# Gathered values: one kernel's V rows by indirect transfers, its weights on a second queue, and a new order

## The chip, the cores and the metric

One core of a Trainium2 chip runs the kernel. The metric is device time in microseconds (us): the median of three timed runs was 982.84 us (980.65 to 984.33). Five engines run side by side, each through its own instruction list in order: TensorE (PE, with its weight loads as PEld), VectorE (DVE), ScalarE (ACT), GpSimd (POOL) and SyncE (SP). Transfers between memory and the on-chip buffers are carried by 16 DMA engines, whichever engine's queue starts them.

## What is computed

Block-sparse attention over 4 batches, 8 heads, 768 positions and 64 channels, followed by an MLP whose gate is h * relu6(h + 3) / 6. A query block of 32 rows sees its own and the two neighbouring blocks, the first and the last block, and three sampled blocks; the first and last query blocks see everything.

```python
mask = np.abs(blk_i - blk_j) <= window                     # window = 1, blocks of 32
mask = mask | (blk_i == 0) | (blk_j == 0) | (blk_i == n_blocks - 1) | (blk_j == n_blocks - 1)
for qb in range(n_blocks):
    for kb in sampled_blocks[qb]:
        mask[qb * block:(qb + 1) * block, kb * block:(kb + 1) * block] = True
scores = np.where(mask, scale * np.matmul(q, k.transpose(0, 1, 3, 2)), -1000000000.0)
attn = softmax(scores)
x = np.matmul(attn, v)                                     # to (tokens, 512)
h = x @ w_in                                               # 512 -> 2048
out = (h * np.clip(h + 3.0, 0.0, 6.0) / 6.0) @ w_out       # 2048 -> 512
```

The weights come as 64-bit floats and the matmuls of the MLP run on a high and a low part, so each weight tile is split on the chip.

## The kernel before, in words

A long table, `SCORE`, writes the whole program out by hand: each entry names a piece of work and its step, and the steps are issued in exactly that order, on the engine that each step uses. Nothing reorders them later, so the table is the order of every queue.

The pieces are these. `k0` is the index: it loads the sampled block numbers and derives a second list for V, in which samples that repeat or lie inside the window are replaced by an empty block. `p0` to `p43` are pairs of neighbouring query blocks: `kw` and `vw` load the four window blocks of K and V, `kg` and `vg` the first and last block (only when the tile held another batch), `kr` and `vr` the six sampled blocks, each by a transfer of its own whose address SyncE takes from a register; `registers` (L342) loads six numbers into registers first. K and V tiles (`kp`, `vp`) form rings of three pairs. `q0` to `q23` load the queries of a group of blocks. `j0` to `j43` are attention jobs: `s` the scores, `mx` the row maximum, `e` the exponentials, `t` transposes, `ca`/`cv` copies, `av` the product with V, `dn`, `ml`, `x`, `xh`, `xl` the division and the split into high and low. `d0` to `d7` are the blocks that see everything, with K and V in tiles named `stage`. `w0` to `w31` are weight tiles: `load` into `stage` (a ring of three), `size` on ScalarE, three `bits` steps on VectorE, `high` on ScalarE, `low` on GpSimd or VectorE, `save` back to memory. `m0` to `m63` are MLP steps, eight units of eight: `h` (24 matmuls), `ga`, `gb`, `gh` and `gl` for the gate and its split into `ghi` and `glo`, `o` (18 matmuls into `out`). The first unit takes the low parts as they are made; later ones load them again with `loadin` and `loadout` (`wlo_in`, a ring of four, and `wlo_out`, a ring of three). After eight steps, `oc` copies and `od` stores the output.

All transfers are started by SyncE (`dma`). Attention runs ahead of the MLP by a few jobs, and both interleave with the weight work in roughly the first quarter of the time. Operations pass through one helper, so nearly every row of the trace carries line L286.

Of the kernel before, what the change touches and what calls it, by code (L numbers as in the profile page):

```python
# [17 lines left out]
P = 128  # L18
# [25 lines left out]
    t_1 ca_0; j2 x; j3 cv_1; j2 xh xl; j3 av_0 av_1 dn; p4 vw; j3 ml; p5 vw; j3 x; p4 vr; j3 xh xl; j4 s; p5 vr; j4 mx
    e_00 e_01 e_10 t_0 e_11; w0 load; j4 cv_0 t_1; w1 load; w2 load; j5 s; j4 cv_1; q3 load; p6 kw kr; j5 mx; j4 av_0;
    j5 e_00; j4 av_1; j5 e_01; j4 dn; j5 e_10 t_0; j4 ml; w0 size; j5 cv_0; j4 x; p7 kw; j5 e_11; p7 kr; w0 bits_0; j4
    xh; j5 t_1; w1 size; w0 bits_1; j5 ca_1; w0 bits_2; j4 xl; w0 high; w1 bits_0; j5 av_0; w0 low_0; w1 bits_1; j5
    av_1; w3 load; p6 vw; w1 bits_2; p7 vw; p6 vr; w2 size; j5 dn ml; w1 high; w2 bits_0; j5 x xh; w2 bits_1; w1
# [696 lines left out]
```

## Time and profile before

| | us |
|---|---|
| median of three runs | 982.84 (980.65 to 984.33) |
| profiled run | 986.81 |
| its span, first to last instruction | 985.0 |
| TensorE busy in the span | 827.3 |
| VectorE busy | 342.2 |
| ScalarE busy | 274.1 |
| GpSimd busy | 152.2 |

An engine's busy time says little by itself, since the stages differ. Which stage an engine waits in, and for whom, is read from the views below: the slices of the span, the table by stage, the chain of work that ended last (followed back from the end, at each step to what released it), and the waits. SPq is SyncE's queue, which starts transfers; "landing" is the end of a transfer.

### The profile page before, as it was taken

The numbers are of one execution on the slowest core, as the hardware profiler recorded it, in microseconds if no ns is written. First come the engines' busy times: TensorE is split into PE (matmuls) and PEld (weight loads), VectorE is DVE, ScalarE is ACT, GpSimd is POOL, SyncE is SP. The second block draws the span as 40 slices with busy tenths as digits, with TensorE's granted clock in tenths as the row PEclk, the third lists the DMA queues.
The fourth block names the chain that finished last, engine by engine and source line by source line (L and its number), as shares of the span: only waits on it lengthen the run. The fifth ranks groups of instructions, "written<-read, shape, count | busy, mean of one in ns | idle before, by whom it ended". The sixth has DMA issues, their size and how long they took to land.

```text
span 985.0 us, 20294 instructions
## 1 busy us (share of the span) xinstructions
PE 827.3 (84%) x7968; PEld 656.8 (67%) x7968; DVE 342.2 (35%) x590; ACT 274.1 (28%) x496; POOL 152.2 (15%) x93
## 2 busy tenths in 40 slices
PE   3567776687899799977998989977999888999997
PEld 1335555565787587756787767756777666778895
DVE  1336566675323143322422223322322223233111
ACT  1114434453223132322222223221232222222121
POOL 0001132231211011110111110110111110111221
PEclk9756877878799799988999989988999999999999
DMA  6557889888665765777457666777456665535441
GB/s 169 163 156 229 264 257 271 230 275 243 214 200 162 212 199 166 225 196 220 151 166 215 197 174 206 223 205 220 141 170 203 186 179 185 156 106 151 143 128 64
DMA packets 134898, 187.71 MB, mean 191 GB/s; under 512 B 16659, under 2 KB 69012, under 8 KB 134804
## 3 DMA queue, kind: packets, MB, share of 16 engines
q1 hardware_dynamic: 134804, 186.43, 63.3%
q8 instruction: 63, 1.03, 0.5%
q14 instruction: 31, 0.25, 0.1%
HBM read 171.68 MB, written 14.68 MB: 189 GB/s over the span
## 4 chain that ended last, share of the span: by engine, by line
PE 54%; SPq 21%; DMA 14%; issue 5%; DVE 5%; ACT 2%; POOL 0%; ACTq 0%; DVEq 0%; POOLq 0%
PE big L286 28%; PE out L286 20%; SPq L286 16%; PE small L286 5%; SPq L342 5%; DMA wlo_out<-wout_lo 4%; DMA stage<-w_out 3%; DMA stage<-w_in 3%; DVE wf L286 2%; DMA out_dram<-wf 1%; DVE pT L286 1%; DMA stage<-vD 1%; DMA kp<-kG 1%; DMA wlo_in<-win_lo 1%; ACT wf L286 1%
## 5 line engine op out<-in xcount | busy, mean ns | idle before, releaser
L286 PE MATMUL big<-x,win_hi 128*128 128x384 f32 x1024 | 282.4, 358 | 14.8 <-DVE g L286 14.6
L286 POOL TENSOR_TENSOR glo<-g,ghi 128x768 fp32r<-128x768 f32 x64 | 118.0, 1843 | 642.5 <-ACT ghi L286 642.5
L286 PEld LDWEIGHTS big<-x,win_hi 128*128 128x128 f32 x1024 | 189.9, 198 | 27.4 <-ACT win_hi L286 9.5
L286 PE MATMUL big<-x,wlo_in 128*128 128x384 f32 x512 | 178.8, 349 | 5.1 <-DMA wlo_in<-win_lo 3.5
L286 PE MATMUL out<-wlo_out,ghi 128*128 128x512 f32 x384 | 156.8, 408 | 28.8 <-DMA wlo_out<-wout_lo 28.8
L286 PE MATMUL out<-wout_hi,ghi 128*128 128x512 f32 x384 | 166.2, 433 | 12.1 <-DVE wf L286 10.3
L286 PE MATMUL out<-wout_hi,glo 128*128 128x512 f32 x384 | 155.9, 406 | 1.3 <-POOL glo L286 1.3
L286 DVE TENSOR_REDUCE m<-big 128x4 f32<-128x1024 f32 (+1 forms) x60 | 68.8, 1151 | 190.2 <-PE big L286 190.2
L286 ACT ACTIVATE g<-big,half_b 128x768 f32<-128x768 f32 x64 | 57.7, 902 | 255.8 <-PE big L286 255.8
L286 ACT ACTIVATE p<-big,m 128x256 f32<-128x256 f32 (+1 forms) x208 | 85.8, 491 | 153.4 <-DVE m L286 147.8
L286 PEld LDWEIGHTS out<-wout_hi,ghi 128*128 128x128 f32 x384 | 75.0, 195 | 48.1 <-issue 16.9
L286 PEld LDWEIGHTS out<-wlo_out,ghi 128*128 128x128 f32 x384 | 75.5, 197 | 46.1 <-DMA wlo_out<-wout_lo 34.8
L286 PEld LDWEIGHTS big<-x,wlo_in 128*128 128x128 f32 x512 | 100.5, 196 | 7.3 <-DMA wlo_in<-win_lo 4.7
L286 DVE COPY pT<-big 128x512 f32<-128x512 f32 (+1 forms) x61 | 46.3, 761 | 143.3 <-PE big L286 137.5
L286 PE MATMUL big<-ident,p 128*128 128x128 f32 x448 | 70.1, 302 | 26.2 <-ACT p L286 23.2
L286 DVE SCALAR_TENSOR_TENSOR g<-g,big 128x768 f32<-128x768 f32 x64 | 60.7, 948 | 82.9 <-ACT g L286 82.9
L286 PEld LDWEIGHTS out<-wout_hi,glo 128*128 128x128 f32 x384 | 75.1, 196 | 20.1 <-POOL glo L286 3.0
L286 PEld LDWEIGHTS big<-ident,p 128*128 128x128 f32 x448 | 56.4, 154 | 40.9 <-ACT p L286 36.4
L286 PE MATMUL big<-kp,q 64*32 64x256 f32 x1408 | 66.4, 436 | 18.9 <-DMA kp<-kG 17.5
L286 PE MATMUL small<-vp,pT 128*32 128x65 f32 x2816 | 62.8, 236 | 14.2 <-DMA vp<-vG 4.9
L286 PEld LDWEIGHTS small<-vp,pT 128*32 128x32 f32 x2816 | 50.6, 118 | 36.2 <-DVE pT L286 13.9
L286 DVE SCALAR_TENSOR_TENSOR wf<-stage,wf 128x512 int32<-128x512 int32 x64 | 62.6, 977 | 2.2
(35 smaller groups left out, 399.0 us busy)
## 6 DMA issues: line engine op xcount, KB each, us to landing
wlo_in<-win_lo SPq DMA_DIRECT2D x112, 256.0 KB, 3.0
wlo_out<-wout_lo SPq DMA_DIRECT2D x112, 256.0 KB, 2.9
vp<-vG SPq DMA_DIRECT2D x44, 390.0 KB, 4.1
vp<-vG SPq DMA_DIRECT2D x264, 65.0 KB, 1.9
kp<-kG SPq DMA_DIRECT2D x44, 384.0 KB, 4.5
kp<-kG SPq DMA_DIRECT2D x264, 64.0 KB, 2.1
stage<-w_in SPq DMA_DIRECT2D x16, 512.0 KB, 4.3
stage<-w_out SPq DMA_DIRECT2D x16, 512.0 KB, 4.4
```

What stands on the lines that cost most here:

```text
L286: return lambda *a, **k: tc.keep_in_program_order(op(*a, **k))
L342: loads, values = nc.values_load_multi_w_load_instructions(row, engines=[mybir.EngineType.SP], min_val=0, max_val=NB - 1, skip_runtime_bou ...
```

## The change

V of a pair is now brought in by four gathers (`vr` with two digits: which block of the pair, which half of the eight key blocks). Each is one indirect transfer on GpSimd's queue that fills 128 partitions: every partition takes the row of V whose number stands in a table `rows`. Window, edge and sampled blocks all come this way, so `vw` and `vg` are gone, and the register loads for V with them. The table is computed once, on VectorE, on 128 partitions, from the sampled numbers and a constant table. V is passed as four arrays, one for each batch, so that a gather's row numbers start at zero.

Loads take a queue number: 0 is SyncE, 1 is ScalarE. ScalarE's queue starts 21 of the 32 weight loads, the first constants, and the K or q of some early pairs. K's sampled blocks keep their transfers with registers, on either queue. Twenty low parts instead of eight are computed by VectorE.

`SCORE` is another table, generated anew. The diff, cut to its core:

```diff
 SCORE = """
-    k0 samp table ident; q0 load; p0 kw; p1 kw; p0 kg; k0 index; p1 kg; p0 kr; p1 kr; p0 vw; p1 vw; p0 vg; p1 vg; p0
+    k0 samp_1 all_0 table_1; q0 load_0; p0 kw_1; p1 kw_0; p0 kg_1; p1 kg_0; k0 ident_1; q1 load_0; p0 kr_1; p1 kr_0;
...
+    queues = (dma, act)
...
-    def registers(row):
-        loads, values = nc.values_load_multi_w_load_instructions(
-            row, engines=[mybir.EngineType.SP], min_val=0, max_val=NB - 1,
-            skip_runtime_bounds_check_because="sampled blocks are numbers of blocks")
-        for x in loads:
-            tc.keep_in_program_order(x)
-        return values
+            dve.tensor_copy(out=self.rows, in_=base)
+            for s in range(NR):
+                at, c = slice((s + 3) % 4 * BLK, (s + 3) % 4 * BLK + BLK), (s + 3) // 4
+                dve.scalar_tensor_tensor(out=self.rows[at, :, c], in0=f3[at, 1:LAST + 1, s], scalar=float(BLK), in1=base[at, :, c], op0=ALU.mult, op1=ALU.add)
...
-        def vw(self):
-            src = vG[self.b]
-            src = bass.AP(src.tensor, src.offset + (self.i - 1) * BLK * VR, [[VR, 3 * BLK], [BLK * VR, 2], [1, VR]])
-            dma.dma_start(out=self.v[:3 * BLK, :, 0], in_=src)
...
-        def vg(self):
-            for j in range(2):
-                dma.dma_start(out=self.v[2 * BLK:, j, 1], in_=vG[self.b, NB * BLK:])
...
-        def vr(self):
-            at = NR * self.i
-            for n, r in enumerate(registers(index.v[:, at:at + 2 * NR])):
-                s = 3 + n % NR
-                src = vG[self.b].rearrange("(n p) w -> n p w", p=BLK)[bass.ds(r, 1)].rearrange("o p w -> (o p) w")
-                dma.dma_start(out=self.v[s % 4 * BLK:(s % 4 + 1) * BLK, n // NR, s // 4], in_=src)
+        def vr(self, j, c):
+            n = self.i - 1 + j
+            pool.indirect_dma_start(out=self.v[:, j, c], out_offset=None, in_=vG[self.b],
+                                    in_offset=bass.IndirectOffsetOnAxis(ap=index.rows[:, n, c:c + 1], axis=0))
...
-        def load(self):
+        def load(self, q):
             self.raw = sb.tile([P, 1024], F32, name="stage", bufs=3).bitcast(I32).rearrange("p (n t) -> p n t", t=2)
-            dma.dma_start(out=self.raw, in_=self.src.bitcast(I32).rearrange("p (n t) -> p n t", t=2))
+            queues[q].dma_start(out=self.raw, in_=self.src.bitcast(I32).rearrange("p (n t) -> p n t", t=2))
```

Three places show what the new table does to the queues. The first is GpSimd's list at steps 23 to 29 of the MLP (each step has one `glo`; `vp0` to `vp2` are the ring of V tiles). Before:

```order
L286 TENSOR_TENSOR glo_5052<-g_5002,ghi_5040 128x768
L286 TENSOR_TENSOR glo_5146<-g_5087,ghi_5136 128x768
L286 TENSOR_TENSOR glo_5227<-g_5208,ghi_5222 128x768
L286 TENSOR_TENSOR glo_5422<-g_5359,ghi_5416 128x768
L286 TENSOR_TENSOR glo_5586<-g_5541,ghi_5580 128x768
L286 TENSOR_TENSOR glo_5702<-g_5642,ghi_5691 128x768
```

And GpSimd's list at the same steps of the changed kernel:

```order
L304 TENSOR_TENSOR glo_4625<-g_4580,ghi_4621 128x768
L304 TENSOR_TENSOR glo_4729<-g_4670,ghi_4719 128x768
L304 TENSOR_TENSOR glo_4810<-g_4791,ghi_4805 128x768
L304 DMA vp1_110<-vG2,rows_173 128x520 x4
L304 DMA vp2_111<-vG2,rows_173 128x520 x4
L304 TENSOR_TENSOR glo_5113<-g_4922,ghi_4981 128x768
L304 TENSOR_TENSOR glo_5185<-g_5161,ghi_5178 128x768
L304 DMA vp0_109<-vG2,rows_173 128x520 x4
L304 TENSOR_TENSOR glo_5352<-g_5247,ghi_5298 128x768
```

The eight gathers of pairs 25 and 26 now stand between the `glo` of step 25 and that of step 26, and pair 27's four before that of step 28.

The second is SyncE's list where a new batch begins (pairs 22 to 24). Before, this is the end of pair 23's V, and what follows:

```order
L286 DMA vp_111<-vG 32x520
L286 DMA wlo_out<-wout_lo_99 128x512
L286 DMA wlo_out<-wout_lo_100 128x512
L286 DMA wlo_in<-win_lo_86 128x512
L286 DMA wlo_in<-win_lo_87 128x512
L286 DMA kp_106<-kG 128x2x384
```

In the changed kernel SyncE has this after the K of pair 23:

```order
L304 DMA kp_108<-kG 128x128
L304 DMA wlo_in<-win_lo_86 128x512
L304 DMA wlo_in<-win_lo_87 128x512
L304 DMA kp_106<-kG 128x2x384
L304 DMA kp_106<-kG 128x2x128 x2
L386 TENSOR_LOAD raw
L304 ISA
```

The 18 V transfers that stood ahead of `wout_lo_99` are gone; the two `wlo_out` loads have moved back behind pair 24's K (six more transfers).

The third is the start of ScalarE's list. Before, it begins with the first job's exponentials:

```order
L286 ACT_TABLE_LOAD
L286 ACTIVATE p<-big,m 128x256 x8
L286 COPY pT<-big 128x512
L286 CAST x_112<-small 128x2x128 x2
L286 ACTIVATE p<-big,m 128x256 x8
```

In the changed kernel ScalarE starts transfers first:

```order
L304 DMA raw<-sampled 1x144
L304 DMA pT<-table 128x116
L304 DMA kp_106<-kG 128x2x384
L304 DMA kp_106<-kG 128x2x128 x2
L304 DMA ident<-ident 128x128
L386 TENSOR_LOAD raw
L304 ISA
```

Constants and K of several early pairs (the sampled blocks of pairs 0, 2, 4 and 5) have moved to ScalarE's queue, ahead of and between its exponentials, and later 21 weight loads.

## Rows read from the trace of the kernel before

**Rows 1.** The page's slices of the span: TensorE, granted clock, DMA engines

```profile
PE   3567776687899799977998989977999888999997
PEclk9756877878799799988999989988999999999999
DMA  6557889888665765777457666777456665535441
```

**Rows 2.** Table by stage: us; busy of PE, PEld, DVE, ACT, POOL; PEclk; DMA share; GB/s

```profile
0.00:100.00 100.00, 57.44 (x782) 33.72 (x790) 36.34 (x74) 22.03 (x47) 4.86 (x8) 0.76 0.65 180
100.00:250.00 150.00, 106.98 (x989) 83.61 (x974) 98.07 (x142) 63.91 (x117) 42.63 (x28) 0.79 0.84 260
...
321.00:973.00 652.00, 591.57 (x5582) 480.80 (x5583) 185.76 (x336) 169.58 (x302) 91.87 (x51) 0.96 0.60 179
...
425.00:465.00 40.00, 28.95 (x218) 22.00 (x213) 8.72 (x17) 5.99 (x10) 3.62 (x2) 0.83 0.73 209
```

**Rows 3.** GpSimd's timeline, 395 to 985 us: start us, us, operation, idle before

```profile
397.12 1.83 POOL L286 TENSOR_TENSOR glo<-g,ghi 128x768 fp32r<-128x768 f32 x1 [10.46 <-ACT ghi L286]
409.41 1.83 POOL L286 TENSOR_TENSOR glo<-g,ghi 128x768 fp32r<-128x768 f32 x1 [10.47 <-ACT ghi L286]
...
922.52 1.85 POOL L286 TENSOR_TENSOR glo<-g,ghi 128x768 fp32r<-128x768 f32 x1 [8.65 <-ACT ghi L286]
930.87 1.85 POOL L286 TENSOR_TENSOR glo<-g,ghi 128x768 fp32r<-128x768 f32 x1 [6.50 <-ACT ghi L286]
```

**Rows 4.** Chain by line, stretches 0 to 100, 100 to 250 and 321 to 985

```profile
by line: SPq L286 56.8%; SPq L342 19.4%; issue 15.8%; PE big L286 1.9%; DMA kp<-kG 1.9%; DMA vp<-vG 1.8%; DVE m L286 1.2%; PE small L286 1.0%; DVE rec L286 0.2%
...
by line: SPq L286 19.5%; DMA stage<-w_out 18.2%; DMA stage<-w_in 16.9%; DVE wf L286 8.5%; issue 6.2%; SPq L342 5.8%; PE big L286 5.4%; DMA kp<-kG 4.6%; ACT wf L286 4.0%; PE out L286 2.7%; DVE m L286 1.7%; ACT g L286 1.5%; POOL wlo_out L286 
...
by line: PE big L286 34.7%; PE out L286 26.7%; SPq L286 10.4%; PE small L286 6.9%; DMA wlo_out<-wout_lo 6.0%; SPq L342 3.5%; issue 3.4%; DMA out_dram<-wf 1.7%; DVE wf L286 1.6%; DMA stage<-vD 1.4%; DVE pT L286 1.4%; DMA wlo_in<-win_lo 1.1%;
```

**Rows 5.** SyncE's timeline, 50 to 76 us (x counts transfers)

```profile
51.90 10.81 SPq L286 DMA_DIRECT2D kp<-kG  x14
62.76 10.39 SPq L286 DMA_DIRECT2D vp<-vG  x14
73.20 0.42 SPq L286 DMA_DIRECT2D stage<-w_in  x1
```

**Rows 6.** SyncE's timeline, 405 to 465 us

```profile
422.17 12.96 SPq L286 DMA_DIRECT2D vp<-vG  x18
435.23 0.84 SPq L286 DMA_DIRECT2D wlo_out<-wout_lo  x2
```

**Rows 7.** Timeline of TensorE's weight loads, 423 to 465 us

```profile
437.92 0.29 PEld L286 LDWEIGHTS out<-wlo_out,ghi 128*128 128x128 f32 x1 [6.13 <-DMA wlo_out<-wout_lo]
...
453.69 1.37 PEld L286 LDWEIGHTS small<-stage,pT 128*64 128x64 f32 x22 [5.31 <-DMA stage<-vD]
```

**Rows 8.** TensorE's waits, 321 to 985 us: us, times, longest

```profile
PE out L286 <- DMA wlo_out<-wout_lo: 28.8, 13, 5.7
PE small L286 <- DMA stage<-vD: 15.0, 3, 5.2
PE out L286 <- DVE wf L286: 8.7, 12, 0.8
...
PE big L286 <- DMA wlo_in<-win_lo: 3.5, 3, 1.9
```

**Rows 9.** Register loads on SyncE, by line: ns min/median/max, first and last start

```profile
L342 SPq TENSOR_LOAD <-raw x44: 1266/1276/2819, 5.4 to 828.1; - x44
```

**Rows 10.** Instructions by tile (wf, wlo, glo): ns min/median/max, first and last start

```profile
L286 DVE SCALAR_TENSOR_TENSOR wf<-stage,wf x64: 691/693/2312, 78.6 to 248.5; 128x512 int32<-128x512 int32 x64
...
L286 POOL TENSOR_TENSOR wlo_out<-wf,wout_hi x14: 1276/1302/1671, 83.8 to 240.1; 128x512 fp32r<-128x512 f32 x14
...
L286 DVE TENSOR_TENSOR wlo_in<-wf,win_hi x6: 678/692/694, 87.3 to 234.1; 128x512 fp32r<-128x512 f32 x6
...
L286 POOL TENSOR_TENSOR glo<-g,ghi x64: 1801/1837/2064, 102.9 to 972.6; 128x768 fp32r<-128x768 f32 x64
```

**Rows 11.** TensorE's timeline, 395 to 410 us: a job's scores

```profile
404.32 1.09 PE L286 MATMUL big<-kp,q 64*32 64x256 f32 x32
```

More of the change, by code (lines that the diff above doesn't have):

```diff
@@ L44 @@
[L44 to L48, printed above, removed]
@@ L262, in fused_kernel @@
 @with_exitstack
-def fused_kernel(ctx: ExitStack, tc, qT, kG, vG, kD, vD, sampled, w_in, w_out, table, ident_d, out):
+def fused_kernel(ctx: ExitStack, tc, qT, kG, vG0, vG1, vG2, vG3, kD, vD, sampled, w_in, w_out, table, ident_d, out):
     nc = tc.nc
@@ L270, in fused_kernel @@
     outp = ctx.enter_context(tc.tile_pool(name="outp", bufs=1, space=bass.MemoryType.PSUM))
+    vG = (vG0, vG1, vG2, vG3)
     def big_tile():
@@ L367, in kg @@
-        def kg(self):
+            queues[q].dma_start(out=self.k[:, :, 0:3].rearrange("p j s n -> p j (s n)"), in_=src)
+        def kg(self, q):
             src = kG[self.b]
             for j in range(2):
-                dma.dma_start(out=self.k[:, j, 6:8], in_=src.rearrange("p (n w) -> p n w", n=NB)[:, ::NB - 1])
-        def vg(self):
-            for j in range(2):
-                dma.dma_start(out=self.v[2 * BLK:, j, 1], in_=vG[self.b, NB * BLK:])
-        def kr(self):
-            at = NR * self.i
-            for n, r in enumerate(registers(index.raw[:, 2 * at:2 * at + 4 * NR:2])):
-                dma.dma_start(out=self.k[:, n // NR, 3 + n % NR], in_=kG[self.b][:, bass.ds(r * (HP * BLK), HP * BLK)])
@@ L381, in vr, with kr @@
-        def vr(self):
-            at = NR * self.i
-            for n, r in enumerate(registers(index.v[:, at:at + 2 * NR])):
-                s = 3 + n % NR
-                src = vG[self.b].rearrange("(n p) w -> n p w", p=BLK)[bass.ds(r, 1)].rearrange("o p w -> (o p) w")
-                dma.dma_start(out=self.v[s % 4 * BLK:(s % 4 + 1) * BLK, n // NR, s // 4], in_=src)
+                queues[q].dma_start(out=self.k[:, j, 6:8], in_=src.rearrange("p (n w) -> p n w", n=NB)[:, ::NB - 1])
+        def kr(self, q):
+            at = 2 * NR * self.i
+            loads, values = nc.values_load_multi_w_load_instructions(
+                index.raw[:, at:at + 4 * NR:2], engines=[mybir.EngineType.Activation if q else mybir.EngineType.SP],
+                min_val=0, max_val=NB - 1, skip_runtime_bounds_check_because="sampled blocks are numbers of blocks")
+            for x in loads:
+                tc.keep_in_program_order(x)
+            for n, r in enumerate(values):
+                queues[q].dma_start(out=self.k[:, n // NR, 3 + n % NR], in_=kG[self.b][:, bass.ds(r * (HP * BLK), HP * BLK)])
@@ L705, in layouts @@
     vg[:, NB + 1] = rows[:, NB - 1]
+    base = np.zeros((4, BLK, LAST, 2), np.int64) + np.arange(BLK)[None, :, None, None]
+    for s in range(3):
+        base[s, :, :, 0] += BLK * (np.arange(LAST) + s)
+    base[2, :, :, 1] += BLK * NB
+    base[3, :, :, 1] += BLK * (NB + 1)
     w_in = np.asarray(moe_w_in).reshape(NKC, P, NF, P).transpose(2, 1, 0, 3).reshape(NF, P, DM)
@@ L710, in layouts @@
         "kG": kb.transpose(0, 2, 5, 3, 1, 4).reshape(B, P, NB * HP * BLK),
-        "vG": vg.reshape(B, (NB + 2) * BLK, VR),
+        **{f"vG{b}": vg[b].reshape((NB + 2) * BLK, VR) for b in range(B)},
         "kD": kb.transpose(0, 1, 2, 5, 3, 4).reshape(B, HP, P, S),
```

398 lines of the change are left out of this document (210 added, 188 removed).

## The prediction

> **What bounds the kernel now.** I read the page's slices first [rows 1]. TensorE stands at 8 or 9 tenths near the end, but at 3 to 8 in the first ten slices, with a granted clock there of mostly 5 to 8 tenths. So the time has two kinds of loss, and the table by stage separates them [rows 2]. [...] From 321 to 973 it is busy 591.6 of 652 us at 0.96: 60.4 us are idle, and some 24 us (4% of 591.6) go to the lowered clock.
>
> What the work costs at full clock comes from GpSimd's one instruction per MLP step, `glo`, used as a stopwatch [rows 3]. Two of them with no attention job between start 8.35 us apart (922.52 to 930.87); with one job between, 12.29 us (397.12 to 409.41). A step is therefore 8.35 us and a job 3.94 us of TensorE. By 250 us seven steps and about 14 jobs are done, 58 + 55 = 113 us of work.
>
> The chain of waits says who causes the loss [rows 4]. Up to 100 us SyncE is 76% of the chain (56.8% issuing, 19.4% loading row numbers into registers), and "issue", the gaps between its instructions, another 16%. From 100 to 250 it is mixed: SyncE 25%, landing of weight tiles 35%, VectorE's bit work 8.5%. From 321 on TensorE itself carries 68%, SyncE still 14%.
>
> SyncE's own timeline prices a pair [rows 5]: K of two pairs takes 10.81 us of queue time, V of two pairs 10.39, and the first weight load leaves only at 73.20 us. So each pair holds the queue for 10.6 us, 5.2 of it for V, and all 44 for 466 us. Later the damage is local. From 422.17 us the V transfers of two pairs and of a new batch's edge blocks hold the queue for 12.96 us, and two `wlo_out` loads wait behind them until 435.23 [rows 6]. The matmul that wants the first starts at 437.92, after 6.13 us idle; a `vD` load behind the next pair's V costs 5.31 us more [rows 7]. Summed over 321 to 985 us TensorE waits 28.8 us for `wlo_out`, 15.0 for `stage<-vD` and 3.5 for `wlo_in`, together 47.3, and 8.7 for VectorE's copies of the output [rows 8].
>
> **SyncE's queue.** V leaves it: 44 x 5.2 = 229 us of queue time removed. K stays, at 5.4 us a pair; early on, the sampled K of four pairs, some windows of K, two q loads and 21 of the 32 weight loads go to ScalarE's queue. That costs ScalarE 58 starts of some 0.42 us [rows 5] and four register loads of 1.27 us [rows 9], 29 us in all; it is busy 86 of the first 250 us [rows 2], so its idle time covers that. Should a start have to wait for its buffer, the Exp and the weight scaling queued behind it wait too, and TensorE behind those.
>
> **The first stage (0 to 250 us).** With that queue free, the DMA engines are late next: 180 GB/s at a share of 0.65 up to 100 us, 260 GB/s at 0.84 from there to 250 [rows 2], 18 + 39 = 57 MB. The changed kernel has about the same to move before the last weight is split. By the shapes in the code a pair's gathers bring 4 x 128 rows of 2080 bytes instead of 384 rows, 0.27 MB more, 4 MB over 15 pairs; some 2 MB go with the edge blocks' own transfers and 1.8 MB of K and q come later in the new order. 57 MB at 260 GB/s from 5 us on end at 224 us. Rings of three V tiles and three stage tiles will hold some loads back, so I take 230, a gain of 20. From it goes what the new order has not done by then: job 12 and the front halves of jobs 13 and 14, about 1.8 jobs or 7 us, and 2 us for a start that first computes row numbers on 128 partitions. Net **11 us**. The ends: at the old mean rate (57 MB in 250 us) nothing is gained and the 9 are lost; at a share of 1.0 (260/0.84 = 310 GB/s) the stage ends near 189 us, net 52. Twelve more low parts move to VectorE (12 x 0.69 us = 8 [rows 10]), which is busy 98 of 150 us [rows 2] and hides them.
>
> **The later stage (321 us on).** If SyncE is on time, the 47.3 us vanish. The clock's mean was 0.83 between 425 and 465 us, the stretch with the two stalls above [rows 2], so I count their share of the clock loss with them, 24 x 47.3/60.4 = 19: at most 66 us. Not all will go: a load issued on time still lands 2.7 us later (435.23 to 437.92), or finds its buffer in use. I take 11 off for that: 55.
>
> **The gathers on GpSimd.** This is the unknown; the trace has no transfer started by GpSimd. It now holds 176 of them in a queue that runs in order, with `glo` behind them, and TensorE's output matmuls wait for `glo`. Bounds for one: a start on SyncE with its share of the register loads, 0.74 us (10.39 over 14) [rows 5], and GpSimd's longest arithmetic, 2.06 us [rows 10]. I take 1.5, near the medians of its own instructions on such tiles, 1.30 (128x512) and 1.84 (128x768) [rows 10]. The cover is counted in the new order: at 11 places eight gathers stand between one `glo` and the next (those of pairs 25 and 26, then step 26's `glo`, are one). The first is released when the preceding job's last V matmul ends. Until step 26's output needs `glo`, TensorE has a step and a job (12.29 us) and the next job's scores (1.09 us [rows 11]): 13.4 us. The queue needs 8 x 1.5 + 1.84 = 13.8 us, 0.4 late at 11 places: **5 us**. At 0.74 us a gather costs nothing; at 2.06 each place is 4.9 late, 54 us. In the first stage 60 gathers (90 us) stand beside some 29 us of GpSimd's arithmetic in 230 us and are covered. The later stage thus gives 55 - 5 = **50 us**.
>
> **Sum.** 985.0 - 11 - 50 = 924 us of span. The profiled run took 986.81 us and the median of the timed runs is 982.84, so the forecast for a median is 982.84 - 61 = **922 us**. About 0.5% is what a measurement of this kernel can tell from no change.
>
> **Rivals.** *Gathers are long and GpSimd becomes the bound.* Everything else gains 11 + 55 = 66 us; 11 x (8T + 1.84 - 13.4) reaches that at T = 2.2 us. Above it each block holds up `glo`, TensorE waits for it at 11 places, and the time passes the old one. At T = 3 each place is 12.4 us late, 137 in all: 985 + 137 - 66 = 1056, a median of 1054; at 2.5, 1010. For it: no row shows GpSimd producing 128 row addresses, and VectorE's two-input bit operation stretches from a median of 0.69 to 2.31 us in the stage in which GpSimd computes too [rows 10]. Against it: a whole pair's V took SyncE 5.2 us, 1.3 per gather with its register loads. [...]
>
> *The first stage is bound by transfers, not by their start.* The DMA engines already stand at 0.84 from 100 to 250 us. If the first 100 us keep their 180 GB/s because buffers, not SyncE, hold the loads back, the first stage loses 9 us and the later one gains 50: 944, a median of 942. Against it: SyncE is three quarters of the chain there [rows 4]. [...]
>
> *The change doesn't free the queue.* K's transfers remain, and where several pairs' K precede a `wlo_out` load it is late as before; waits of TensorE for late V take the rest: a median of 975 to 987.
>
> *More than forecast.* The DMA engines come near a share of 1.0 early, some 30 us more: 880 to 900.
>
> **How the numbers follow.** Forecast (905 to 942) 0.50; first stage bound by transfers (942 to 960) 0.14; more than forecast 0.08; queue not freed 0.07; GpSimd the bound (988 to 1060) 0.21. To hold eight in ten the range takes in the first four and a little of the last: 880 to 990. Faster by over 0.5% 0.72, within 0.5% 0.07, slower 0.21.
>
> **What would show it.** Right: SyncE's share of the chain up to 100 us well below 76%, a DMA share above 0.75 there, the last weight split near 230 us, TensorE's waits for `wlo_out` and `vD` together under 15 us, gathers 1.5 us apart where nothing holds them. Wrong: TensorE or its weight loads waiting for `glo` in tens of us, gathers over 2.2 us apart, or the last weight split no earlier than 250 us.

## The result and the profile after

The changed kernel takes 967.12 us (median of 3, 966.62 to 967.25) against 982.84: a ratio of 0.984 (95% interval 0.981 to 0.987). The forecast was 922. The time went down, and inside the range of 880 to 990, but by 16 us instead of 61.

This time depends on the session. In some sessions the other engines are held up for some microseconds while GpSimd sends several gathers in a row (5.3 us in the row shown below), in others not, with one and the same program (e8 and e16 below, 937.51 and 873.48 us). The result above comes from a session with these stalls. The sections below say how that was found and what each part of the change is worth with and without them.

The table by stage, as in [rows 2], from 0 to 100, 100 to 250, and 321 us to the last `glo`:

```profile
0.00:100.00 100.00, 37.26 (x608) 22.72 (x608) 40.62 (x82) 28.02 (x58) 31.41 (x36) 0.85 0.77 251
100.00:250.00 150.00, 122.94 (x1282) 99.35 (x1282) 97.21 (x158) 61.53 (x110) 65.02 (x52) 0.92 0.77 254
321.00:953.00 632.00, 588.54 (x5461) 468.21 (x5460) 180.19 (x326) 166.44 (x295) 181.06 (x146) 0.96 0.59 183
```

The DMA engines move 251 GB/s in the first 100 us instead of 180, VectorE already does more there than before (40.62 us for 36.34), but TensorE's mean clock in the later stage is 0.96 as before. The chain of waits of the first 100 us, as in [rows 4]:

```profile
by line: DMA kp<-kG 23.6%; another core or an unknown queue 13.3%; issue 9.3%; DVE wf L304 8.7%; PE big L304 8.4%; PE small L304 5.9%; DMA q<-qT 4.9%; DMA stage<-w_out 4.0%; SPq L304 3.5%; DVE m L304 3.0%; ACT p L304 2.2%; DVE xq L304 1.7%;
```

SyncE's issuing (`SPq L304`) falls from 56.8% to 3.5%. New is an entry of 13.3% for which the profile finds no releaser. By tile, VectorE's bit work (against [rows 10]) and the gathers, ns min/median/max and first to last start:

```profile
L304 DVE SCALAR_TENSOR_TENSOR wf<-stage,wf x64: 679/693/2286, 45.4 to 219.8; 128x512 int32<-128x512 int32 x64
...
L304 POOL DMA_INDIRECT vp<-vG,rows x176: 942/949/1347, 8.4 to 813.5; - x176
```

The last weight is split at 219.8 us instead of 248.5. A gather takes 0.95 us of GpSimd, and GpSimd's timeline below shows 0.30 us between two: 1.25 us each. TensorE's waits from step 13 on (307 to 965 us), as in [rows 8]:

```profile
PE big L304 <- ACT p L304: 12.5, 10, 3.2
PE big L304 <- issue: 11.7, 25, 1.0
PE out L304 <- DVE wf L304: 9.9, 14, 0.8
PE out L304 <- issue: 4.2, 8, 0.8
...
PE out L304 <- DMA wlo_out<-wout_lo: 0.4, 1, 0.4
PE out L304 <- POOL glo L304: 0.2, 1, 0.2
```

The 47 us of waits for weight tiles and dense V are gone but for 0.4, and for `glo` TensorE waits 0.2 us. So every sign that the prediction named as right is there, and yet the later stage is hardly shorter. GpSimd's timeline gives its length, as in [rows 3]; steps 13 and 63:

```profile
306.94 1.84 POOL L304 TENSOR_TENSOR glo<-g,ghi 128x768 fp32r<-128x768 f32 x1 [3.81 <-ACT ghi L304]
...
952.86 1.84 POOL L304 TENSOR_TENSOR glo<-g,ghi 128x768 fp32r<-128x768 f32 x1 [6.53 <-ACT ghi L304]
```

From step 13 to step 63 before took 651.9 us (320.7 to 972.6), now it takes 645.9. Up to step 13 the change gained 13.8 us, behind it 6.0. Where the rest is shows in three timelines around one row of eight gathers. GpSimd first (start us, us, operation, idle before it):

```profile
361.94 0.96 POOL L304 DMA_INDIRECT vp<-vG,rows  x1 [0.87 <-PE small L304]
363.20 0.95 POOL L304 DMA_INDIRECT vp<-vG,rows  x1 [0.30 <-issue]
...
370.72 0.95 POOL L304 DMA_INDIRECT vp<-vG,rows  x1 [0.30 <-issue]
377.43 1.83 POOL L304 TENSOR_TENSOR glo<-g,ghi 128x768 fp32r<-128x768 f32 x1 [5.76 <-ACT ghi L304]
```

TensorE beside it:

```profile
366.38 1.82 PE L304 MATMUL big<-kp,q 64*32 64x256 f32 x32
369.05 0.48 PE L304 MATMUL out<-wout_hi,ghi 128*128 128x512 f32 x1 [0.84 <-issue]
369.37 0.40 PE L304 MATMUL out<-wlo_out,ghi 128*128 128x512 f32 x1
370.46 0.39 PE L304 MATMUL out<-wout_hi,glo 128*128 128x512 f32 x1 [0.70 <-issue]
```

VectorE beside it:

```profile
361.94 0.16 DVE L304 TENSOR_SCALAR rec<-small 128x4 f32<-128x4 f32 x1 [1.48 <-PE small L304]
...
363.77 0.42 DVE L304 TENSOR_TENSOR x<-small,x 128x256 fp32r<-128x256 f32 x1 [1.00 <-issue]
373.53 1.23 DVE L304 TENSOR_REDUCE m<-big 128x4 f32<-128x1024 f32 x1 [9.33 <-remote]
```

A job's 32 score matmuls, 1.09 us in [rows 11], are spread over 1.82. Between output matmuls that have all their data TensorE stands idle for "issue", 0.84 and 0.70 us. And VectorE's reduction of the scores, which ended at 368.20, starts at 373.53, 5.3 us after its input was there and 1.9 us after the last gather of the row ended (371.67). The trace has ten such rows of seven or eight gathers from 250 us on. In all ten VectorE starts nothing between 4 us after the row's first start and 1.7 to 2.6 us after its end, while TensorE goes on with what it has. From one `glo` to the next (359.23 to 377.43) this step with one job takes 18.2 us instead of the 12.29 of [rows 3].

### The profile page after: what moved, and what is told of

It reads as the page before. It is cut to its first block, busy times and chain, and to the rows that moved or that the text cites. A ratio compares the mean times of both kernels' runs of the same rounds, so it can differ in the third digit from the quotient of the medians.

```text
span 965.5 us, 19549 instructions
## 1 busy us (share of the span) xinstructions
PE 819.0 (85%) x7968; PEld 642.9 (67%) x7968; DVE 340.2 (35%) x605; ACT 274.6 (28%) x496; POOL 304.9 (32%) x257
## 4 chain that ended last, share of the span: by engine, by line
PE 70%; DVE 11%; issue 6%; DMA 5%; another core or an unknown queue 3%; ACT 3%; SPq 1%; ACTq 0%; POOL 0%; POOLq 0%
PE big L304 38%; PE out L304 24%; PE small L304 7%; DVE wf L304 5%; DMA kp<-kG 3%; DVE m L304 3%; ACT p L304 2%; DVE pT L304 2%; DMA stage<-w_out 1%; DVE g L304 1%; SPq L304 1%; DMA stage<-w_in 1%; DMA q<-qT 1%; ACT wf L304 0%
## 5 line engine op out<-in xcount | busy, mean ns | idle before, releaser
L304 PE MATMUL big<-x,win_hi 128*128 128x384 f32 x1024 | 276.9, 352 | 13.1 <-issue 6.3
L304 POOL TENSOR_TENSOR glo<-g,ghi 128x768 fp32r<-128x768 f32 x64 | 118.0, 1844 | 453.8 <-ACT ghi L304 453.6
L304 POOL DMA_INDIRECT vp<-vG,rows x176 | 170.6, 969 | 133.9 <-PE small L304 81.5
L304 PEld LDWEIGHTS big<-x,win_hi 128*128 128x128 f32 x1024 | 184.1, 193 | 27.4 <-issue 20.2
L304 PE MATMUL out<-wout_hi,ghi 128*128 128x512 f32 x384 | 167.9, 437 | 14.0 <-DVE wf L304 11.4
L304 PE MATMUL big<-x,wlo_in 128*128 128x384 f32 x512 | 175.5, 343 | 3.3 <-DVE wlo_in L304 1.4
L304 PE MATMUL out<-wout_hi,glo 128*128 128x512 f32 x384 | 156.6, 408 | 3.3 <-issue 1.9
L304 PE MATMUL out<-wlo_out,ghi 128*128 128x512 f32 x384 | 156.4, 407 | 2.2 <-issue 1.6
L304 DVE TENSOR_REDUCE m<-big 128x4 f32<-128x1024 f32 (+1 forms) x60 | 68.8, 1152 | 244.3 <-PE big L304 134.2
L304 ACT ACTIVATE p<-big,m 128x256 f32<-128x256 f32 (+1 forms) x208 | 86.6, 493 | 186.2 <-DVE m L304 153.5
L304 ACT ACTIVATE g<-big,half_b 128x768 f32<-128x768 f32 x64 | 57.9, 904 | 251.2 <-PE big L304 204.4
L304 PE MATMUL big<-ident,p 128*128 128x128 f32 x448 | 71.0, 304 | 60.4 <-ACT p L304 57.0
L304 PEld LDWEIGHTS out<-wout_hi,ghi 128*128 128x128 f32 x384 | 75.6, 197 | 51.9 <-issue 20.8
L304 PEld LDWEIGHTS big<-ident,p 128*128 128x128 f32 x448 | 56.7, 156 | 77.4 <-ACT p L304 69.5
L304 DVE COPY pT<-big 128x512 f32<-128x512 f32 (+1 forms) x61 | 46.3, 761 | 159.8 <-PE big L304 152.6
L304 PEld LDWEIGHTS big<-x,wlo_in 128*128 128x128 f32 x512 | 98.6, 193 | 4.1 <-DVE wlo_in L304 2.1
L304 PE MATMUL big<-kp,q 64*32 64x256 f32 x1408 | 73.0, 417 | 32.1 <-issue 15.1
L304 PEld LDWEIGHTS out<-wout_hi,glo 128*128 128x128 f32 x384 | 75.1, 196 | 21.9 <-POOL glo L304 2.2
L304 DVE SCALAR_TENSOR_TENSOR g<-g,big 128x768 f32<-128x768 f32 x64 | 60.7, 948 | 79.8 <-ACT g L304 79.8
L304 PEld LDWEIGHTS out<-wlo_out,ghi 128*128 128x128 f32 x384 | 75.6, 197 | 17.3 <-issue 4.2
L304 PEld LDWEIGHTS big<-kp,q 64*32 64x32 f32 x1408 | 27.1, 112 | 63.6 <-issue 55.0
L304 PEld LDWEIGHTS small<-vp,pT 128*32 128x32 f32 x2816 | 47.5, 117 | 25.8 <-DVE pT L304 14.1
```

Source lines behind the costliest of these rows:

```text
L304: return lambda *a, **k: tc.keep_in_program_order(op(*a, **k))
```

## Experiments

"Step 13" stands for the start of step 13's `glo`, "13 to 63" for the time from there to step 63's. A session ran up to four kernels on one chip, each of the five sessions on another chip. "Landings" are the transfer completions that the trace holds, of those that were due (16 for each transfer, as in before: 16,660 for 1,043 transfers).

| run | us, median | ratio to before, 95% | step 13 | 13 to 63 | landings |
|---|---|---|---|---|---|
| before | 982.84 | | 320.7 | 651.9 | 16,660 of 16,688 |
| changed | 967.12 | 0.984 [0.981, 0.987] | 306.9 | 645.9 | 9,978 of 14,144 |
| session 1: e1, V by SyncE | 986.64 | 1.003 [1.000, 1.006] | 316.9 | 656.6 | 16,690 of 16,704 |
| e2, old order | 892.58 | 0.909 [0.902, 0.916] | 295.2 | 584.1 | 14,069 of 14,144 |
| e3, one queue | 887.59 | 0.903 [0.897, 0.909] | 273.4 | 599.3 | 14,018 of 14,144 |
| e4, old order from step 11 | 878.60 | 0.893 [0.888, 0.898] | 279.8 | 583.4 | 14,057 of 14,144 |
| session 2: e5, changed | 963.02 | 0.977 [0.971, 0.983] | 302.2 | 645.6 | 9,857 of 14,144 |
| e6, weights on ScalarE | 957.65 | 0.971 [0.965, 0.977] | 296.1 | 646.8 | 9,839 of 14,144 |
| e7, K and q on ScalarE | 962.73 | 0.975 [0.970, 0.981] | 306.1 | 644.0 | 9,832 of 14,144 |
| e8, as e4, one queue | 937.51 | 0.948 [0.941, 0.955] | 298.6 | 625.3 | 9,758 of 14,144 |
| session 3: e9, changed | 977.71 | 0.993 [0.991, 0.996] | 312.1 | 652.5 | 9,823 of 14,144 |
| e10, four at a time | 975.38 | 0.992 [0.988, 0.996] | 312.8 | 644.3 | 10,298 of 14,144 |
| e11, short gathers | 1044.05 | 1.061 [1.055, 1.068] | 321.9 | 709.4 | 9,207 of 14,144 |
| e12, none later | 909.05 | 0.924 [0.919, 0.929] | 302.5 | 590.7 | 10,867 of 12,416 |
| session 4: e13, half the rows | 893.52 | 0.907 [0.900, 0.914] | 282.6 | 596.6 | 14,010 of 14,144 |
| e14, spare gathers | 996.23 | 1.011 [1.003, 1.019] | 326.2 | 653.4 | 19,325 of 19,520 |
| e15, two a pair | 902.73 | 0.918 [0.912, 0.924] | 282.2 | 601.6 | 14,785 of 14,848 |
| e16, as e8 | 873.48 | 0.887 [0.882, 0.892] | 273.2 | 581.0 | 14,037 of 14,144 |
| session 5: e17, changed | 970.09 | 0.990 [0.984, 0.996] | 304.7 | 643.4 | 9,872 of 14,144 |
| e18, two a pair | 907.44 | 0.922 [0.919, 0.926] | 290.8 | 606.3 | 12,968 of 14,848 |

The theory after the result was that the new order costs the later stage what the gathers gain (the waits for `p` had grown to 12.5 us, from 1.1 in before); its rival was that the gathers' traffic holds up K. The first session takes the parts of the change apart.

**e1_new_order_v_on_sync.** A pair's V comes by SyncE again, at the place of its first gather.

```diff
         def vr(self, j, c):
-            pool.indirect_dma_start(out=self.v[:, j, c], out_offset=None, in_=vG[self.b],
-                                    in_offset=bass.IndirectOffsetOnAxis(ap=index.rows[:, n, c:c + 1], axis=0))
+            if (j, c) != (0, 0):
+                return
+            dma.dma_start(out=self.v[:3 * BLK, :, 0], in_=src)
...
+                dma.dma_start(out=self.v[x % 4 * BLK:(x % 4 + 1) * BLK, n // NR, x // 4], in_=src)
```

> The new order and ScalarE's queue stay, but V comes by SyncE's transfers as before (a window, the edge blocks where the pair has them, six blocks by register), all of a pair's at the place of its first gather. If the gathers carry the gain, SyncE's queue binds again: the later stage's waits for weight tiles and dense V return and the time is 980 to 1010 us. If the new order and the second queue carry it, the time stays at 962 to 972.

Measured 986.64 us. Without the gathers the other two parts of the change gain nothing.

**e2_gathers_old_order.** The changed kernel with before's order: the four gathers stand where the window of V was loaded, all loads go to SyncE.

```diff
-    k0 samp_1 all_0 table_1; q0 load_0; p0 kw_1; p1 kw_0; p0 kg_1; p1 kg_0; k0 ident_1; q1 load_0; p0 kr_1; p1 kr_0;
+    k0 samp_0 all_0 table_0 ident_0; q0 load_0; p0 kw_0; p1 kw_0; p0 kg_0; k0 index; p1 kg_0; p0 kr_0; p1 kr_0; p0
...
```

> V by gathers, but in the order of before (a pair's four gathers where its window of V was loaded) and every load on SyncE's queue. Theory order: the new order loses in the later stage (scores that wait for K, Exp tiles without MLP matmuls beside them) what the gathers gain; with the old order step 13 to step 63 takes 605 to 620 us instead of 646 and the whole 925 to 945. Theory traffic: the bursts of gathers hold up K's transfers in any order; 955 to 970.

**e3_one_queue.** Every queue number of the changed order is 0.

```diff
-    k0 samp_1 all_0 table_1; q0 load_0; p0 kw_1; p1 kw_0; p0 kg_1; p1 kg_0; k0 ident_1; q1 load_0; p0 kr_1; p1 kr_0;
+    k0 samp_0 all_0 table_0; q0 load_0; p0 kw_0; p1 kw_0; p0 kg_0; p1 kg_0; k0 ident_0; q1 load_0; p0 kr_0; p1 kr_0;
...
```

> The changed kernel with all loads on SyncE's queue. If ScalarE's queue gives the first stage its gain of 14 us, step 13 starts 10 to 14 us later and the time is 977 to 982. If the gathers alone give it, the time stays at 965 to 970.

**e4_old_order_from_step_11.** The changed order up to `j14 xl`, before's from there; at job 28, for instance, `m31 gl` stands ahead of pair 30's gathers again, and step 31's output matmuls between the job's scores and its transposes.

```diff
...
-    m32 h_10; p30 vr_00; m32 h_01; p30 vr_01; m32 h_11; m34 loadin_0; j28 s; m34 loadin_1; p30 vr_10; j28 mx; p30
-    vr_11; j28 e_00 e_01 e_10; m31 gl; j28 e_11 t_0 t_1 cv_0 ca_1; m31 o_00; m32 ga; j28 av_0 av_1; m32 gb; m31 o_01;
+    xh; m31 gh; j27 xl; m30 o_11; m31 gl; m30 o_20 o_21; m32 h_00; m31 loadout_1; p30 vr_00 vr_01 vr_10 vr_11; m32
+    h_10 h_01 h_11 loadout_0; j28 s; m33 loadin_0; m32 ga; m33 loadin_1; m34 loadin_0; m31 o_00; j28 mx; m34 loadin_1;
+    m31 o_01 o_10; m32 gb; j28 e_00 e_01; m31 o_11; j28 e_10; m31 oc_0; j28 e_11; m31 o_20; m32 gh; m31 oc_1 od_0; j28
+    t_0; m32 loadout_1; m31 od_1; m32 gl; j28 t_1 cv_0; m31 o_21; j28 ca_1 av_0; m33 loadout_0; j28 av_1; m31 oc_2;
...
```

> The new order up to the end of job 14 (step 11 of the MLP), from there on the order of before, V by gathers throughout. Theory order: the first stage keeps its gain and the later one runs in 605 to 620 us, in all 925 to 940. Theory traffic: 955 to 968, as the changed kernel.

Measured 892.58, 887.59 and 878.60 us: all three far below every expectation, and e3 80 us below the changed kernel, from which it differs in the queue of 58 early loads, 37 of K, q and constants and 21 of weights. Up to step 13 the new order alone is worth 21.8 us (e2 295.2, e3 273.4); behind it, it loses 15 to 16 (e3 599.3, e2 584.1, e4 583.4). The same stretch of e3 as shown above for the changed kernel, VectorE and then TensorE:

```profile
331.73 0.42 DVE L304 TENSOR_TENSOR x<-small,x 128x256 fp32r<-128x256 f32 x1 [1.00 <-ACT x L304]
335.56 1.23 DVE L304 TENSOR_REDUCE m<-big 128x4 f32<-128x1024 f32 x1 [3.40 <-PE big L304]
```

```profile
334.35 1.09 PE L304 MATMUL big<-kp,q 64*32 64x256 f32 x32
335.37 0.49 PE L304 MATMUL out<-wout_hi,ghi 128*128 128x512 f32 x1
```

Here the scores are whole, end at 335.44, and the reduction starts 0.12 us later, although eight gathers run from 329.90 to 338.66 as in the changed kernel. What separates the two is not that stretch of the program. Either ScalarE's queue early on has effects 100 us later, or the session is another. The second session asks that.

**e5_changed_again.** No edit.

> The changed kernel itself, unaltered, in the same session as the three below. If what separates it from the variant with one load queue (887.6 us against 967.1) lies in the program, it takes 962 to 972 us again, and step 18 to step 22 of the MLP 56 us. If it lies in that one session, it takes 880 to 900, and those steps about 50.

**e6_weights_on_scalare** and **e7_k_q_on_scalare.** ScalarE's queue for the weights alone, and for all but the weights.

```diff
-    xl; w3 load_1; j2 mx; w0 high; j1 av_0 av_1; w0 low_0; j1 dn; j2 e_00; j1 ml; j2 e_01; p3 vr_00; w1 bits_0; w0
+    xl; w3 load_0; j2 mx; w0 high; j1 av_0 av_1; w0 low_0; j1 dn; j2 e_00; j1 ml; j2 e_01; p3 vr_00; w1 bits_0; w0
...
```

That is a line of e7; in e6 these stay 1 and those of `k`, `p` and `q` become 0.

> The changed kernel with only the 21 weight loads on ScalarE's queue; K, q and the small early loads go to SyncE. If the second queue as such costs the time (both queues count on the same eight completion semaphores), it stays near 967 us. If only the early K and q on ScalarE cost it, 885 to 895. If the queue costs nothing, as the run just above.

> The changed kernel with only the early K, q, table and sampled rows on ScalarE's queue, the weight loads all on SyncE's. If the weights on ScalarE cost the time, 880 to 895 us; if the early K does, near 967.

**e8_old_order_later_one_queue.** e4 with the queue numbers of e3.

> New order up to job 14, old order behind it, all loads on SyncE's queue. Steps 0 to 13 as in the variant with one queue (step 13 starts at 273 us), steps 13 to 63 as with the old order (583 us), then 13 us: a span of 870 and a time of 872 us. If the early stage needs ScalarE's queue, 879 or more.

Measured 963.02, 957.65, 962.73 and 937.51 us, while before took 985.35, as ever. e8, with no load on ScalarE's queue, has the stalls too and in e16 (session 4) ran without them in 873.48. So the session decides, not the queue: 13 to 63 takes 644 to 647 us in e5 to e7 and 599.3 in e3, with one and the same order. In the sessions with stalls the trace also lacks 27 to 35% of the landings (13% where gathers are left out, e12 and e18), in the others 1% at most; before and e1, which have no gathers, lack next to none. The third session asks what of the gathers it is.

**e9_changed_third_session.** No edit.

> The changed kernel itself in one more session, beside which the next three are read. In the first two sessions (967.1 and 963.0 us) every engine stood still for a while whenever GpSimd sent seven or eight gathers in a row; in the session of the variants with one queue none did, and they took 886 to 893. Theory: the stalls are all that separates the two; then it takes either 958 to 970 with the step from gather to gather at 12 to 18 us where eight stand in a row, or 880 to 895 without.

**e10_four_gathers_at_a_time.** 60 gathers move behind the next `glo`; those of pairs 17 and 18 for instance, three of them past step 12's:

```diff
...
-    o_11; j16 e_10 e_11; m11 o_20; m12 gh; j16 t_0; p17 vr_11; j16 t_1 cv_0; m11 o_21; j16 ca_1; m12 gl; j16 av_0
+    ca_1; m12 gl; p17 vr_10; p18 vr_10; p17 vr_11; j16 av_0 av_1; m12 loadout_1; m13 h_00; j16 dn; m13 loadout_0; j16
...
```

> Wherever more than four gathers stand between one glo and the next on GpSimd, the later ones (60 of 176, from step 2 of the MLP on) go behind that glo, so that a row holds four. Theory burst: the stalls come from rows of eight and vanish; where the changed kernel takes 960, this takes 880 to 900, and where it takes 885, it takes 880 to 890. Theory bytes: each gather costs the same however spread; within 1% of the changed kernel.

Measured 975.38 beside e9's 977.71, which itself lies above the 958 to 970 expected of it. Step 17 to 18, with a row of four, now takes 13.0 us instead of e9's 18.3, but the next step, with the other four, takes 18.9; together 31.9, in e9 30.9 (364.4 to 395.3). So the sum stays, but the two rows differ in their place. The first starts when the job's V matmuls have ended, as in the changed kernel. The second follows `glo`, and those matmuls end inside it:

```profile
380.05 0.96 POOL L302 DMA_INDIRECT vp<-vG,rows  x1
...
382.15 0.23 PE L302 MATMUL small<-vp,pT 128*32 128x65 f32 x1 [0.45 <-issue]
...
383.81 0.95 POOL L302 DMA_INDIRECT vp<-vG,rows  x1 [0.30 <-issue]
385.90 0.16 DVE L302 TENSOR_SCALAR rec<-small 128x4 f32<-128x4 f32 x1 [6.46 <-remote]
```

VectorE's `rec` takes what the V matmuls wrote. Here it starts 3.5 us after the last of them and 1.1 us after the row; in the changed kernel it starts 0.15 us after the last (361.79 to 361.94), as the row starts. The run moves 60 of the gathers to a worse place, so it doesn't refute that long rows make the stalls; it shows that the place of a row counts too.

**e11_short_gathers.**

```diff
-            pool.indirect_dma_start(out=self.v[:, j, c], out_offset=None, in_=vG[self.b],
+            out, rows = self.v[:, j, c], vG[self.b]
+            if self.n >= 17:
+                out, rows = out[:, :VW], rows.rearrange("r (h w) -> (r h) w", w=VW)
+            pool.indirect_dma_start(out=out, out_offset=None, in_=rows,
```

> From pair 17 on each gather brings 65 instead of 520 columns (260 bytes a row, 128 rows as before), so the output of those pairs differs. Theory bytes: with an eighth of the bytes the later stalls go (steps 17 to 18 and 33 to 34 of the MLP take 12.4 us instead of 18.2), in all 895 to 910 where the changed kernel takes 960. Theory count: descriptors and starts are as many as before, the stalls stay, 950 to 960.

Measured 1044.05, above both expectations. The bytes are not the cause: with an eighth of them the stalls are there, and longer, 24.4 us from step 17 to 18. Nor is it the packets. The page counts 8,896 on the gathers' queue, 80 for each of the 68 long gathers and 32 for each of the 108 short ones. A stretch of the trace with all engines (start us, us, engine, operation, idle before), and the table by stage:

```profile
375.79 1.31 PE L304 MATMUL small<-vp,pT 128*32 128x65 f32 x48
...
376.20 0.96 POOL L304 DMA_INDIRECT vp<-vG,rows  x1
...
384.97 0.95 POOL L304 DMA_INDIRECT vp<-vG,rows  x1 [0.30 <-issue]
387.65 0.16 DVE L304 TENSOR_SCALAR rec<-small 128x4 f32<-128x4 f32 x1 [12.17 <-remote]
...
388.63 0.66 PE L304 MATMUL small<-ident,xq 128*128 128x128 f32 x2 [9.95 <-DVE xq L304]
```

```profile
380.00:385.00 5.00, 0.00 (x0) 0.00 (x0) 0.00 (x0) 0.00 (x0) 3.78 (x5) 0.64 0.53 155
```

TensorE's V matmuls end at 377.10; `rec` starts at 387.65, 10.5 us later and 1.7 us after the row's last gather (385.92). From 380 to 385 us no engine but GpSimd executes anything. But the edit also moved the row. A short gather overwrites the 65 columns of one head, and here the first starts 0.9 us before the V matmuls end, where the changed kernel's waits for them (0.87 us in its first row above). So `rec` has the whole row ahead of it, as in the worse half of e10. That explains the longer stalls without the length of a transfer; whether shorter transfers add to them isn't shown.

**e12_no_gathers_later.**

```diff
+            if self.n >= 17:
+                return
             n = self.i - 1 + j
```

> From pair 17 on no gathers at all, so those pairs use V of earlier ones and the output differs. If the gathers are what stalls the engines, steps 13 to 63 take 590 to 600 us on any chip, 895 to 910 in all where the changed kernel takes 960. If the new order costs the time, they stay at 646.

Measured 909.05, inside the 895 to 910 of the first theory: 13 to 63 takes 590.7 us instead of e9's 652.5. Of the gathers left out 96 fall into it, on average 61.8 / 96 = 0.64 us for each. That is an average and not the price of one gather: it is a whole row that holds up VectorE (step 17 to 18 takes 18.3 us instead of 12.2). Forty steps (13 to 53) of e9 and of e12, in the table by stage:

```profile
312.00:868.00 556.00, 507.99 (x5008) 400.21 (x5004) 164.99 (x304) 148.36 (x273) 164.59 (x137) 0.95 0.61 190
```

```profile
303.00:796.00 493.00, 473.33 (x5000) 383.22 (x5002) 164.44 (x304) 147.98 (x272) 72.90 (x40) 1.00 0.53 163
```

In the same forty steps TensorE is idle for 48 us with the gathers and 20 without, and busy for 35 us more, at a mean clock of 0.95 against 1.00. e3 without stalls, 273 to 776 us:

```profile
273.00:776.00 503.00, 480.11 (x5017) 386.74 (x5017) 165.52 (x304) 148.63 (x273) 164.28 (x136) 0.99 0.66 212
```

Where nothing stalls, the gathers cost little: 503 us with all of them against 493 with none.

**e13_half_the_rows** and **e14_spare_gathers.**

```diff
+            up = 64 if self.n >= 17 else P
-            pool.indirect_dma_start(out=self.v[:, j, c], out_offset=None, in_=vG[self.b],
-                                    in_offset=bass.IndirectOffsetOnAxis(ap=index.rows[:, n, c:c + 1], axis=0))
+            pool.indirect_dma_start(out=self.v[:up, j, c], out_offset=None, in_=vG[self.b],
+                                    in_offset=bass.IndirectOffsetOnAxis(ap=index.rows[:up, n, c:c + 1], axis=0))
```

```diff
+    spare = const.tile([P, 4, 104], F32, name="spare")
...
         def vr(self, j, c):
+            pool.indirect_dma_start(out=spare[:, 2 * j + c], out_offset=None, in_=vG[self.b].rearrange("r (h w) -> (r h) w", w=104),
+                                    in_offset=bass.IndirectOffsetOnAxis(ap=index.rows[:, self.i - 1 + j, c:c + 1], axis=0))
             if (j, c) != (0, 0):
                 return
```

> From pair 17 on each gather fetches 64 rows instead of 128 (partitions 0 to 63; the rest of V keeps older rows, so the output of those pairs differs). Without them steps 13 to 53 of the MLP took 494 us, with them 556, so a gather costs 0.6 us. If the cost goes with the rows, steps 13 to 53 take 520 to 530; if with the starts, 550 to 560; if shorter transfers make it worse, as 260-byte rows did (613), above 570. In a session without stalls all three are 495 to 505.

> The new order with V by SyncE's transfers (986.6 us without gathers), and 176 gathers of 416-byte rows into a spare tile that nobody reads. If gathers cost all engines 0.6 to 1.1 us each whatever waits for them, 1080 to 1170 us; if their cost lies in who waits for V, 985 to 1000. In a session without stalls 985 to 1000 too.

Session 4 met no stalls, so e13 (893.52 us) doesn't tell rows from starts, and e14 (996.23) doesn't tell its two theories apart. 176 gathers that nobody reads, beside V on SyncE's queue, leave 13 to 63 at 653.4 us (656.6 in e1, in another session); up to step 13 they go with 9.3 us more. In these two, without stalls, the gathers show no price in the later stage; what unread gathers do with stalls was not run.

**e15_two_gathers_a_pair** and **e16_old_order_later_again.** e15 is e8 with the window of V and its first sampled blocks by SyncE; the two gathers with `c` = 1 stay. e16 is e8 without an edit.

```diff
         def vr(self, j, c):
             n = self.i - 1 + j
+            if c == 0:
+                if j == 0:
+                    self.window()
+                return
...
+        def window(self):
...
+            dma.dma_start(out=self.v[:3 * BLK, :, 0], in_=src)
...
+                dma.dma_start(out=self.v[3 * BLK:, n, 0], in_=src)
```

> Old order from job 14 on and one load queue, but a pair's window of V and its first two sampled blocks come by SyncE (3 transfers), and only the two gathers that hold the other sampled blocks and the edge blocks stay on GpSimd. If the cost goes with the number of gathers, half of some 80 us comes back against the run below, less what SyncE's 2.8 us more per pair costs: 15 to 35 us faster than it. If SyncE's queue binds again, 10 to 30 slower. In a session without stalls it is 0 to 20 slower.

> The run of the second call with the new order up to job 14, the old one behind it and one load queue, for the comparison above: 937 us as there if the engines stall at gathers, about 870 if not.

Measured 902.73 and 873.48 us: 29 us slower than four gathers, more than the 0 to 20 expected without stalls. The last session takes it to another chip.

**e17_changed_fourth_session** (no edit) and **e18_two_gathers_again** (e15 unedited).

> The changed kernel itself. In a session without stalls 883 to 897 us: steps 13 to 53 of the MLP in 502 us as in the variant with one queue, step 13 at 273 to 285. In one with stalls 960 to 980.

> The variant with two gathers a pair (902.7 us in a session without stalls). With stalls, half of the 60 to 80 us that four gathers cost come on top: 925 to 945, still below the changed kernel's 960 to 980 and about the 937 of four gathers in the old order. Without stalls 897 to 908 again.

Session 5 met the stalls: the changed kernel takes 970.09 us, and two gathers a pair 907.44, below its expectation. With half the gathers nearly all of the stalls go, not half: 13 to 63 takes 606.3 us with and 601.6 without them. That fits e10 and e11: from step 17 on no row has more than four gathers, and each starts after the V matmuls. It beats before in either kind of session, and the changed kernel where there are stalls. Without stalls the changed kernel itself was never run; e13, which differs from it in half the rows of later gathers, takes 893.52 and is faster. Four gathers in e8's order are faster still without stalls (873.48) and 30 us slower with them (937.51).

**What stays open.** Why some sessions stall. That fewer bytes don't help (e11, 24.4 us from step 17 to 18 with an eighth of them), that VectorE waits until a row is over (1.7 to 2.6 us past its end in the changed kernel), and that 27 to 35% of the landings are missing from the same traces, speaks against the traffic of the data as the cause; it is argued, not shown. Whether a signal comes late or VectorE itself is held isn't told apart either. Every time in this document comes with a record of its run, so whether the recording plays a part is not shown. Whether it is the chip or the session is open too, since each of the five sessions had another chip. Whether the price goes with a gather's rows or its start wasn't settled (e13 met no stalls).

## Why the prediction was right or wrong

The path of 61 us, as it was forecast and as the runs show it. The gain without stalls and ScalarE's queue is e3's, ScalarE's price is e4 against e3 up to step 13, the stalls are the changed kernel against e4 up to step 13 and against e3 behind it, so they take in whatever else differs between two sessions.

| | forecast | without stalls, one queue | ScalarE's queue | stalls | measured |
|---|---|---|---|---|---|
| up to step 13 | 11 | 47.3 | -6.4 | -27.1 | 13.8 |
| 13 to 63 | 50 | 52.6 | | -46.6 | 6.0 |

**SyncE's queue: right in what it frees, wrong in what ScalarE's starts cost.** `SPq` leaves the chain, and e1 shows that without this the rest gains nothing. The 29 us of ScalarE's starts were counted at nothing. They cost 6.4 us up to step 13 (e4 279.8, e3 273.4), and by all signs it is the early K and q: in session 2 e7, with these on ScalarE, reaches step 13 at 306.1 and e8, with nothing there, at 298.6; e6, with only the weights there, at 296.1. These are single traces, and e5, with both there, has 302.2. The sentence on the Exp that waits behind a start was the right one, and no price was put on it. With both on it, ScalarE's queue saves nothing in these runs.

**The first stage: a number that is right for wrong reasons.** 11 us were forecast and 13.8 came. But without stalls step 13 comes 47.3 us earlier, near the end of 52 that stood for DMA engines at a share of 1.0. What failed here is "57 MB at 260 GB/s", with its allowance for rings of tiles: in e3 the DMA engines move 283 GB/s from 0 to 198.5 us, at a share of 0.86. That is 56 MB, so the amount was right and the rate too low. The last weight is split at 198.5 us, not 230:

```profile
L304 DVE SCALAR_TENSOR_TENSOR wf<-stage,wf x64: 680/693/2481, 36.0 to 198.5; 128x512 int32<-128x512 int32 x64
```

**The later stage without the gathers: right.** 55 us were forecast, and e12, without them, gains 61.2 (651.9 to 590.7), with the waits gone and the clock at 1.00. It would be more with the old order: e4 takes 583.4 and e16 581.0 us, so the new order costs 16 us here. TensorE's waits in e16 from 273 us on:

```profile
PE big L298 <- ACT p L298: 2.5, 6, 0.5
```

against 8.4 us in e3 for the same tile, 7.3 of them in two waits of 3.65: with `glo` behind eight gathers, the new order has no output matmuls to put between a job's scores and its transposes. These waits are 5.9 of the 16 us; the rest wasn't traced.

**The gathers on GpSimd: the step that failed.** The term was 8 x 1.5 + 1.84 against a cover of 13.4 us, 5 us in all. Its parts were nearly right: 1.25 us a gather instead of 1.5, inside the bounds of 0.74 and 2.06, and no wait for `glo` to speak of. The number of places was too high: from step 13 on seven rows of eight and two of seven stand between one `glo` and the next, not 11 of eight, which makes the term 3 us. What it left out is that a gather could cost anybody but GpSimd and those who wait for it. In the session of the result the gathers hold up the engines beside GpSimd, VectorE until a row is over, and those that wait for VectorE: 46.6 us from step 13 on (96 gathers, 0.49 us each on average) and 27.1 before. No row of before could show it, since GpSimd starts no transfer there; but the bounds for the unknown were drawn for one engine alone, and that was a choice. With the stalls' price in it, the sum is 47.3 - 6.4 - 27.1 + 52.6 - 46.6 = 19.8 us, and the span fell by 19.5; it closes because the stalls are what is left over. That gathers are their cause is shown by e12, that a session can be free of them by e8 and e16.

**The rivals.** "Gathers are long" had the right place and the wrong path: its price ran through gathers longer than 2.2 us. Beside VectorE's bit work, up to 220 us, the gathers have a median of 0.95 us and take 1.35 at most, behind it 0.95 and 1.01; and e3 with the same bit work has no stalls. "More than forecast" (880 to 900) is what happens where no engine stalls: e3 takes 887.59 and e13, but for half the rows of its later gathers the changed kernel, 893.52. The forecast of 922 lies between the two kinds of session and was met in neither; that the result fell into the range of 880 to 990 is luck, since its gains and losses were other ones.

**The signs.** All those that were named as right came true (a share of SyncE far below 76%, a DMA share of 0.77, a last split at 219.8 us, waits of 0.4 us, gathers 1.25 us apart), and the time was wrong. They asked whether the named mechanisms work; none asked whether a matmul with all its data starts at once.

## What to carry to other kernels

When a change brings a kind of instruction that the trace does not contain, its price has two parts, what it takes on its own engine and what it does to all others; leaving it out of a stretch, as e12 does, measures both in one run (61.8 us for 96 gathers). When such a run moves anything else, say where its instructions now stand: e10 and e11 changed the place of a row beside its length or its bytes, and the place decided. Where the other engines show idle time with no releaser ("issue", "remote"), compare the producer's end with the consumer's start before blaming the order. And time a program in more than one session before its order is tuned to what one of them shows: two gathers a pair, the rest by plain transfers, was the version whose time differed by 0.5% between a session with stalls and one without (907.44 and 902.73 us).

## What the hardware showed that was not expected

- A gather of 128 rows of 2080 bytes takes GpSimd a median of 0.95 us (1.35 at most in the changed kernel), and in a row the next starts 0.30 us later, with stalls and without (e3); with 260 bytes a row (e11) it is 0.95 us too, and with 64 rows (e13) little less: from step 13 to 53 GpSimd is busy 159.84 us, in e3 164.28.
- In four of six sessions (the result's and the five above) the changed kernel takes 643 to 653 us from step 13 to 63. In the result's, VectorE starts 5.3 us after its input is there when that falls into a row of eight gathers, and 1.9 us after the row; in e11, of another of the four, it is 10.5 and 1.7. In e3, of one of the two others, it is 0.12 us after its input.
- The kernel before, which has no gathers, took 982.7 to 986.1 us in all five sessions.
